# Earlier double casts and a regrouped set-up in a lightweight convolution followed by a maxout layer

## The chip, the cores and the metric

The kernel runs on one core of one Trainium2 chip. The metric is the device time of one execution in microseconds. Ten runs of the kernel before had a median of 466.01 us (464.97 to 468.08).

## The reference

Two layers follow each other. The first is a causal convolution over seven tokens with one row of seven softmax weights for each of eight heads of 24 channels; the second takes the largest of three products and multiplies it by an output matrix:

```
w   = softmax(weight, axis=-1)                  # 8 heads x 7 taps
y   = sum over k of w[h, k] * x[b, s + k - 6, h, :]   # zeros before a sequence
h   = max(y @ w1, y @ w2, y @ w3)               # 192 -> 768
out = h @ w_out                                 # 768 -> 192
```

x has 8 sequences of 4160 tokens with 192 channels in float32, so 33,280 tokens; the output has the same shape.

## The kernel before

**Blocks.** The tokens are cut into 65 blocks of 512 (eight for each sequence, and one block of the eight remainders of 64). For each block there are four kinds of work. *Load and cast*: `load_x` (L139) brings a block of x into one of seven float32 buffers (`xf`; from block 11 on only three of them, those of blocks 4, 5 and 6, take turns), and `cast_x` (L180) makes fp16 of it on POOL, into a tile `x16`. A tile `x16` holds block 4 alone, then two blocks each, and from block 13 (`QUADS`) on four. *Convolution*: `conv` (L347) multiplies bands of the taps (`band`) with `x16` on TensorE; a quad's convolution is done in two halves of four heads, in the blocks four and three ahead of the quad's first. `evac` brings it from PSUM to `ys`, `turn` transposes it by DMA into `yp`, `double` (L418) copies each half of `yp` to the other 64 partitions on POOL. *Layer 1*: `l1` (L496) makes for each block six tiles of 128 hidden channels. Since max(a, b, c) = max(a - c, b - c, 0) + c, it only needs y times (w1 - w3) and (w2 - w3), the matrices `wd`; `top` takes their larger, with a Relu on ACT and a max on DVE. The part c @ w_out becomes y times one small matrix, m = w3 @ w_out (`m16`). *Output*: `st2` (L530) multiplies h with `wo` and y with `m16`, ACT and DVE add the two lanes, `store` writes 384 KB.

**The loop.** Block t does layer 1 of block t and the output of block t - 1, interleaved. A table made ahead of the loop, `casts`, says up to which block x is cast at the start of block t; a second, `loads`, says up to which block x is loaded in block t. `casts` rises by one for each block, and by two at the blocks that a condition names (L682); `loads` follows `casts` (L683). In block t, `cast_x` stands at its start (L700); the loads stand behind the convolution's transposes on the SP queue if block t has a convolution ("late"), and otherwise behind the store of block t - 2. Each queue runs in the order in which the code was written: nothing overtakes. The convolutions stand at blocks 2, 3, 4, 6, 8, then 9 and 10 (quad 13 to 16), 13 and 14 (quad 17 to 20), and so on.

**The set-up.** The first four blocks go another way: `cast_dense` (L200) casts their x into `xz`, and `conv_dense` (L366) makes the convolution in one piece, y in `yd`, without a transpose. Its two halves, n = 0 for channels 0 to 127 and n = 1 for the rest, go to two PSUM tiles. `l1_dense` (L515) makes tiles of layer 1 for blocks 0 and 1: a "full" product over 128 rows (L522), then a "half" one over 64 rows for each lane (L526). `make_wd` (L295) subtracts w3 from w1 and w2, `copy_w3` and `cast_w3` prepare w3, `transpose_w3` (L321) transposes it on TensorE, `make_m` (L331) multiplies it with `wo`. `zero_x` (L128) clears partitions of the x buffers that no load writes. The set-up ends with the first output products of block 0 (`st2`), block 2's `conv_dense` and `make_m`; the loop's first block then has block 3's `conv_dense`.

Of the kernel before, what the change touches and what calls it, by code (L numbers as in the profile page):

```python
# [10 lines left out]
FP32 = mybir.dt.float32  # L11
FP16 = mybir.dt.float16
# [3 lines left out]
P = 128  # L16
# [12 lines left out]
def kernel(  # L29
# [95 lines left out]
        assert all(v[0] is not xf for v in xin.values())  # L125
        xin[t] = [xf, 0, ()]

    def zero_x(t):  # L128

        if t >= NDENSE:  # L130
            get_x(t)
        xf = xbuf[t]
        q0 = 0 if t >= NDENSE else NQ
        zero = idle[TOK:HALF, 0:D]
        nc.scalar.copy(out=xf[TOK:HALF, q0:NR, :],
                       in_=bass.AP(tensor=zero.tensor, offset=zero.offset,
                                   ap=[list(zero.ap[0]), [0, NR - q0], [1, D]]))

    def load_x(t, eng=nc.sync):  # L139
        if not 0 <= t < NB:  # L140
# [147 lines left out]

    w3h = const.tile([P, 2, DFF], FP16)
    wd = const.tile([P, NC + 1, DFF], FP16)  # L290
    w3t = const.tile([P, NJ, D], FP16)
    wo = const.tile([P, NJ, D], FP16)
    m16 = const.tile([P, 2, D], FP16)

    def make_wd(n, j0, j1, eng=nc.vector):  # L295
        f = slice(P * j0, P * j1)
        eng.tensor_sub(out=wd[:, n, f], in0=ws[:, n, f], in1=w3s[:, n // 2, f])
# [23 lines left out]
    def transpose_w3(g):  # L321
        ps = psw.tile([P, 2, D], FP32, tag="w", name=f"pt{g}")
        for k in range(2):
            js = slice(P * (2 * g + k), P * (2 * g + k + 1))
            for n in range(2):
                row = slice(0, HALF if n else P)
                nc.tensor.matmul(ps[:, k, P * n:min(P * (n + 1), D)], lhsT=w3h[row, n, js],
                                 rhs=ident16[row, row], start=True, stop=True)
        nc.scalar.copy(out=w3t[:, 2 * g:2 * g + 2, :], in_=ps[:])

    def make_m(i):  # L331

        ps = psp.tile([P, D], FP32, tag="p", name=f"pm{i}")
        for j in range(NJ):
            if i == 0:
                nc.tensor.matmul(ps[:], lhsT=w3t[:, j, 0:P], rhs=wo[:, j, :],
                                 start=(j == 0), stop=(j == NJ - 1))
                continue
            for e in range(2):
                nc.tensor.matmul(ps[HALF * e:HALF * (e + 1), :], lhsT=w3t[:, j, P:D],  # L340
                                 rhs=wo[:, j, :], start=(j == 0), stop=(j == NJ - 1))
        nc.scalar.copy(out=m16[:, i, :], in_=ps[:])


# [21 lines left out]
            slots[t0] = ysp.tile([P, 2, nu, 2, D], FP16, tag="ys", name=f"ys_{t}")  # L366
        convs[t0] = G, heads[0]

    def conv_dense(t, copies, pools=((None, None),) * 2):


        yd = dense[t] = ydp.tile([P, NC, NBLK], FP16, tag="yd", name=f"yd_{t}")
        for n, slots_ in enumerate(((0, 1, 2, 3), (4, 5, 4, 5))):
            pool, tag = pools[n]
            ps = (pool or psw).tile([P, NBLK], FP32, tag=tag or "w", name=f"D{n}_{t}")
            for (q, b, row_lo, rlen, lo, hi, cc) in chunks_of[t]:
                for v in range(2):
                    for g, s in enumerate(slots_):
                        h = (32 * s + 31 * v) // GRP
                        nc.tensor.matmul(  # L380
                            ps[32 * g:32 * g + 32, lo:hi],
                            lhsT=xz[t][v][0:rlen, q, 32 * s:32 * s + 32],
                            rhs=band[0:rlen, h, cc:cc + hi - lo],
                            start=(v == 0), stop=(v == 1), tile_position=(0, 32 * g))
            copies[n](out=yd[:, 2 * n, :], in_=ps[:])
# [49 lines left out]
    def y_all(t, i, c):  # L435
        if t < NDENSE:
            return dense[t][HALF * i:HALF * (i + 1), side(i, c), :]
        a = y_row(t, i)
        s0, s1, s2, s3 = (spot(t, i, c, r) for r in range(4))
        assert s3 - s2 == s1 - s0  # L440
        return bass.AP(tensor=a.tensor, offset=a.offset + P * s0,
                       ap=[list(a.ap[0]), [P * (s2 - s0), 2], [P * (s1 - s0), 2], [1, P]])
# [69 lines left out]
        op(lambda: top(t, j, ps))  # L512
        emit()

    def l1_dense(tiles):  # L515

        meet()
        ps = {}
        for t, j, pools in tiles:
            for i, (pool, tag) in enumerate(pools):  # L520
                ps[t, j, i] = pool.tile([P, NBLK], FP32, tag=tag, name=f"l{tag}{i}_{t}_{j}")
                nc.tensor.matmul(ps[t, j, i][:], lhsT=wd[:, i, P * j:P * (j + 1)], rhs=dense[t][:, 0, :],  # L522
                                 start=True, stop=False)
        for t, j, _ in tiles:
            for i in range(2):
                nc.tensor.matmul(ps[t, j, i][:], lhsT=w_of(i, NC - 1, j), rhs=y_all(t, i, NC - 1),  # L526
                                 start=False, stop=True)
        return [lambda t=t, j=j: top(t, j, (ps[t, j, 0], ps[t, j, 1])) for t, j, _ in tiles]

    def st2(t, upto):  # L530

# [89 lines left out]
    WW = ((psw, "w"), (psw, "w"))  # L621
    WPWQ = ((psw, "w"), (psp, "p"), (psw, "w"), (psq, "q"))
    ACT, DVE = nc.scalar.copy, nc.vector.tensor_copy
    make_wd(0, 0, 2)
# [17 lines left out]
    copy_w3(ACT, 2, 6)  # L642
    make_wd(2, 2, 6)
    a, b = l1_dense([(1, 0, WW), (1, 1, PQ)])
    cast_w3(2, 6)
    a()
    b()
    transpose_w3(0)
    nc.gpsimd.tensor_copy(out=wo[:], in_=wos[:])
    cast_dense(2, (nc.gpsimd.tensor_copy, nc.gpsimd.tensor_copy))  # L650
    for f in l1_dense([(0, 2, PQ), (0, 3, WW)]):
        f()
    zero_x(0)
    for f in l1_dense([(1, 2, PQ), (1, 3, WW)]):
        f()
    zero_x(1)
    transpose_w3(1)
    for f in l1_dense([(0, 4, PQ), (0, 5, WW)]):
        f()
    transpose_w3(2)  # L660
    for f in l1_dense([(1, 4, WW), (1, 5, PQ)]):
        f()
# [115 lines left out]
```

## Time and profile before

| | |
|---|---|
| median of ten runs | 466.01 us |
| the profiled execution, its own time | 467.33 us |
| its span, first to last instruction | 465.5 us |
| mean granted TensorE clock | 0.987 |
| TensorE (PE) busy | 451.7 us, 97% |
| VectorE (DVE) busy | 358.7 us, 77% |
| ScalarE (ACT) busy | 322.6 us, 69% |
| GpSimd (POOL) busy | 200.5 us, 43% |
| queue of data transfers | 70.75 MB, 65.1% of 16 engines' span |
| queue of instructions | 61 packets, 1.00 MB |

All times in a profile count from the first instruction. PE is the matmul, PEld the load of its weights, SPq the queue on which SyncE issues DMAs. In a row of the timeline the columns are start, duration, engine, line, operation, the tiles (written <- read), the shape of written <- read, and how many; in brackets stands how long the engine was idle before it and what ended that. "Issue" there means that the profile shows nothing that the engine waited for. In a row of stretches the columns are the stretch, its length, the busy time (and number) of PE, PEld, DVE, ACT and POOL, the mean granted clock, the share of the DMA engines' time and GB/s. In a row of waits stand the total, how often, and the longest.

### The profile page before, as it was taken

Reading aid. Unit: us, or ns where it says so; the run is one execution under the profiler, and the core shown is the slowest. Engines: PE = TensorE matmul, PEld = TensorE weight load, DVE = VectorE, ACT = ScalarE, POOL = GpSimd, SP = SyncE. Lnnn points to the kernel's source line nnn. Section 1 sums busy time; section 2 is a strip of 40 time slices with the busy share of each in tenths; the row PEclk is TensorE's granted clock in tenths of the full one; section 3 lists DMA queues with packets and bytes.
Section 4 is the critical chain, followed back from the end, with each engine's and each line's share of the span. In section 5 each row is a group of like instructions: output and inputs, shape, how many; then the busy total and the mean of one; then the engine's idle time right before and its main releaser. Section 6 shows DMA issues by size and latency. Waiting matters only on the chain.

```text
span 465.5 us, 18644 instructions
## 1 busy us (share of the span) xinstructions
PE 451.7 (97%) x7764; PEld 415.3 (89%) x7764; DVE 358.7 (77%) x616; ACT 322.6 (69%) x610; POOL 200.5 (43%) x223
## 2 busy tenths in 40 slices
PE   8989999499999999999999999999999999999996
PEld 4369999499999999999999999999999999999996
DVE  7657877387878888787878788787887878787775
ACT  8836767266767777676767777676777767676664
POOL 2564356606546353445446452444545361425000
PEclk9989999799999999999999999999999999999999
DMA  7938967549595866949496875959487664924223
GB/s 201 216 72 189 193 163 188 147 110 226 131 188 159 180 167 145 179 135 211 119 174 158 173 189 120 187 143 213 126 158 184 155 177 117 180 77 107 60 68 105
DMA packets 127988, 72.04 MB, mean 155 GB/s; under 512 B 52064, under 2 KB 127711, under 8 KB 127903
## 3 DMA queue, kind: packets, MB, share of 16 engines
q1 hardware_dynamic: 127743, 70.75, 65.1%
q8 instruction: 61, 1.00, 1.0%
q14 instruction: 24, 0.20, 0.2%
q10 hardware_dynamic: 160, 0.10, 0.1%
HBM read 33.28 MB, written 25.56 MB: 126 GB/s over the span
## 4 chain that ended last, share of the span: by engine, by line
PE 93%; DMA 2%; issue 1%; DVE 1%; ACT 1%; POOL 0%; SPq 0%; DVEq 0%; POOLq 0%
PE po L574 35%; PE lq L505 30%; PE lp L505 21%; PE G L360 3%; DMA xf<-in_x_dram 2%; PE D L380 1%; ACT r L492 1%; PE lp L522 0%; POOL x L192 0%; PE lw L522 0%; PE lq L522 0%; PE lp L526 0%; DVE yd L391 0%; PE lw L526 0%; DVE xz L209 0%
## 5 line engine op out<-in xcount | busy, mean ns | idle before, releaser
L574 PE MATMUL po<-wo,h 64*128 64x192 f16 x3120 | 336.8, 243 | 0.1
L493 DVE TENSOR_TENSOR h<-r,lq 128x512 f16<-128x512 f16 x385 | 264.0, 686 | 89.2 <-ACT r L492 79.8
L492 ACT ACTIVATE r<-lp 128x512 f16<-128x512 f32 x385 | 229.9, 597 | 114.5 <-PE lp L505 102.6
L505 PE MATMUL lp<-yp,wd 64*128 64x512 f16 x1098 | 296.7, 377 | 0.0
L505 PE MATMUL lq<-yp,wd 64*128 64x512 f16 x1098 | 296.3, 377 | 0.0
L574 PEld LDWEIGHTS <-h 64*128 64x128 f16 x3120 | 246.9, 94 | 7.1 <-issue 4.9
L505 PEld LDWEIGHTS <-wd 64*128 64x128 f16 x2268 | 179.7, 94 | 11.8 <-issue 0.3
L192 POOL CAST x<-xf 103x768 f16<-103x768 f32 x122 | 97.5, 827 | 127.0 <-DMA xf<-in_x_dram 124.8
L574 PE MATMUL po<-m,yp 64*128 64x192 f16 x732 | 143.7, 244 | 0.0
L422 POOL COPY yp<-yp 64x1536 f16<-64x1536 f16 (+1 forms) x62 | 89.6, 1445 | 85.4 <-DMA yp<-ys 35.2
L584 DVE TENSOR_TENSOR o<-a,po 128x384 f32<-128x384 f32 (+1 forms) x132 | 71.3, 541 | 0.6 <-ACT a L583 0.6
L574 PEld LDWEIGHTS <-yp 64*128 64x128 f16 x732 | 67.5, 94 | 0.3
L583 ACT COPY a<-po 128x384 f32<-128x384 f32 (+1 forms) x132 | 61.6, 468 | 1.4 <-PE po L574 1.1
L399 ACT CAST ys<-G 128x384 f16<-128x384 f32 x61 | 26.3, 482 | 18.5 <-PE G L360 18.5
L399 DVE CAST ys<-G 128x384 f16<-128x384 f32 x61 | 31.0, 550 | 5.7 <-PE G L360 5.7
L360 PE MATMUL G<-x,band 39*32 39x192 f16 (+2 forms) x1152 | 17.7, 238 | 5.9 <-POOL x L192 5.9
L360 PEld LDWEIGHTS <-band 39*32 39x32 f16 x1152 | 11.0, 93 | 10.8 <-issue 10.8
L505 PE MATMUL lq<-yd,wd 64*128 64x512 f16 x36 | 10.3, 391 | 0.3 <-DVE yd L391 0.3
L505 PE MATMUL lp<-yd,wd 64*128 64x512 f16 x36 | 10.2, 391 | 0.0
L380 PEld LDWEIGHTS <-xz 112*32 112x32 f16 x320 | 4.9, 111 | 3.9 <-issue 2.2
L209 POOL CAST xz<-xf 112x240 f16<-112x240 f32 (+2 forms) x15 | 4.4, 333 | 8.9 <-DVE w3s L301 7.6
L380 PE MATMUL D<-band,xz 112*32 112x103 f16 (+1 forms) x320 | 5.8, 236 | 2.0 <-issue 1.9
(62 smaller groups left out, 87.1 us busy)
## 6 DMA issues: line engine op xcount, KB each, us to landing
xf<-in_x_dram SPq DMA_DIRECT2D x113, 234.0 KB
out_dram<-o SPq DMA_DIRECT2D x62, 384.0 KB
xf<-in_x_dram SPq DMA_DIRECT2D x7, 204.8 KB
xf<-in_x_dram SPq DMA_DIRECT2D x3, 420.0 KB
ws<-in_moe_w_dram SPq DMA_DIRECT2D x8, 128.0 KB
yp<-ys SPq DMA_TRANSPOSE x62
out_dram<-o SPq DMA_DIRECT2D x5, 192.0 KB
wos<-in_moe_w_out_dram SPq DMA_DIRECT2D x1, 576.0 KB
```

Of the source, the lines that this page charges most:

```text
L192: nc.gpsimd.tensor_copy(out=x16s[t0][0:K, :, :, u, r, :].rearrange("p h j c -> p j h c"), in_=xf[0:K, 4 * r:4 * r + 4, :].rearrange("p j ( ...
L209: copy(out=xz[t][v][0:rl, q0:q1, :].rearrange("p q (k c) -> p q k c", c=CYC)[:, :, :, a:b], in_=xf[0:rl, q0:q1, :].rearrange("p q (k c) -> ...
L360: nc.tensor.matmul(G[2 * (k // per) + i][TOK * j:TOK * (j + 1), k % per, :], lhsT=band[row, h, HALF * i + LAP:HALF * i + KR], rhs=x16s[t0] ...
L380: nc.tensor.matmul(ps[32 * g:32 * g + 32, lo:hi], lhsT=xz[t][v][0:rlen, q, 32 * s:32 * s + 32], rhs=band[0:rlen, h, cc:cc + hi - lo], star ...
L399: copy(out=slots[t][:, i % 2, :, :, GRP * h0:GRP * (h0 + per)].rearrange("p u r (h c) -> p h (u r) c", c=GRP), in_=G[i][:].rearrange("p h ...
L422: nc.gpsimd.tensor_copy(out=yp[HALF * i:HALF * (i + 1), 1, :, :, :, :].rearrange("p i u k n -> p (i u k n)"), in_=yp[HALF * (1 - i):HALF * ...
L492: nc.scalar.activation(out=r[:], in_=ps[0][:], func=AF.Relu)
L493: nc.vector.tensor_max(out=hs[t][:, j, :], in0=r[:], in1=ps[1][:])
L505: nc.tensor.matmul(ps[i][:], lhsT=w_of(i, c, j), rhs=y_all(t, i, c), start=(n == 0), stop=(n == NC - 1))
L574: nc.tensor.matmul(ps[b0, i][:, s % 2, :], lhsT=a, rhs=b, start=first, stop=last and (t > 0 or s % 2 == 1))
L583: nc.scalar.copy(out=a[:, ss, :], in_=ps[s0, 0][:, ss, :])
L584: nc.vector.tensor_add(out=outs[t][:, s0:s + 1, :], in0=a[:, ss, :], in1=ps[s0, 1][:, ss, :])
```

## The change

There are two parts.

**Casts and loads.** The blocks at which two blocks of x are cast instead of one are 6, 7 and 8, where they were 8 and 9. `casts` becomes 9, 10, 12, 14, 16, 17, 18 at blocks 4 to 10, from 9, 10, 11, 12, 14, 16, 17, and `loads` follows it: 10, 12, 14, 16, 17 at blocks 4 to 8, from 10, 11, 12, 14, 16. So the x of blocks 13 to 16, the first quad, is cast at blocks 7 and 8, and from block 9 on all casts and loads stand one block earlier.

**Set-up.** `l1_dense` can now make its full and half products in any order (`parts`), and keeps its PSUM tiles open between calls; `tops` does the Relu and max afterwards. The sequence of calls is written anew: full and half products of neighbouring calls stand together, `transpose_w3` and `conv_dense` can begin with either half, block 2's `conv_dense` stands ahead of `st2` of block 0, and copies and subtractions change engines. `transpose_w3` writes 128 instead of 64 columns for its second half, twice the same 64 (`w3t` is wider), so that `make_m` needs 6 products with full columns for its second half, where it had 12.

```diff
-    def zero_x(t):
+    def zero_x(t, q0=0, q1=NR, eng=None):
...
-        q0 = 0 if t >= NDENSE else NQ
+        if eng is not None:
+            eng.memset(xf[TOK:HALF, q0:q1, :], 0.0)
+            return
...
-    w3t = const.tile([P, NJ, D], FP16)
+    w3t = const.tile([P, NJ, 2 * P], FP16)
...
+    def transpose_w3(g, order=(0, 1)):
+        ps = psw.tile([P, 2, 2 * P], FP32, tag="w", name=f"pt{g}")
+        for n in order:
+            row = slice(0, HALF if n else P)
+            for k in range(2):
+                js = slice(P * (2 * g + k), P * (2 * g + k + 1))
+                unit = ident16[row, row]
+                if n:
+                    unit = bass.AP(tensor=unit.tensor, offset=unit.offset,
+                                   ap=[list(unit.ap[0]), [0, 2], [1, HALF]])
+                nc.tensor.matmul(ps[:, k, P * n:P * (n + 1)], lhsT=w3h[row, n, js],
+                                 rhs=unit, start=True, stop=True)
         nc.scalar.copy(out=w3t[:, 2 * g:2 * g + 2, :], in_=ps[:])
...
         for j in range(NJ):
-            if i == 0:
-                nc.tensor.matmul(ps[:], lhsT=w3t[:, j, 0:P], rhs=wo[:, j, :],
-                                 start=(j == 0), stop=(j == NJ - 1))
-                continue
-            for e in range(2):
-                nc.tensor.matmul(ps[HALF * e:HALF * (e + 1), :], lhsT=w3t[:, j, P:D],
-                                 rhs=wo[:, j, :], start=(j == 0), stop=(j == NJ - 1))
+            nc.tensor.matmul(ps[:], lhsT=w3t[:, j, P * i:P * (i + 1)], rhs=wo[:, j, :],
+                             start=(j == 0), stop=(j == NJ - 1))
...
-    def conv_dense(t, copies, pools=((None, None),) * 2):
+    def conv_dense(t, copies, pools=((None, None),) * 2, order=(0, 1)):
...
-        for n, slots_ in enumerate(((0, 1, 2, 3), (4, 5, 4, 5))):
+        for n in order:
+            slots_ = ((0, 1, 2, 3), (4, 5, 4, 5))[n]
...
+    def l1_dense(tiles, parts="FH"):
 
         meet()
+        for n, part in enumerate(parts):
+            for t, j, pools in tiles:
+                for i, (pool, tag) in enumerate(pools):
+                    if (t, j, i) not in open_ps:
+                        open_ps[t, j, i] = pool.tile([P, NBLK], FP32, tag=tag, name=f"l{tag}{i}_{t}_{j}")
+                        begun.discard((t, j, i))
+                    if part == "F":
+                        a, b = wd[:, i, P * j:P * (j + 1)], dense[t][:, 0, :]
+                    else:
+                        a, b = w_of(i, NC - 1, j), y_all(t, i, NC - 1)
+                    nc.tensor.matmul(open_ps[t, j, i][:], lhsT=a, rhs=b,
+                                     start=(t, j, i) not in begun, stop=(t, j, i) in begun)
+                    begun.add((t, j, i))
...
     make_wd(1, 0, 2)
+    zero_x(6, 4, NR, nc.vector)
     conv_dense(0, (ACT, DVE))
-    zero_x(6)
+    zero_x(6, 0, 4)
...
-    cast_dense(1, (nc.gpsimd.tensor_copy, ACT))
-    a, b = l1_dense([(0, 0, PQ), (0, 1, PQ)])
+    cast_dense(1, (GP, ACT))
+    make_wd(0, 2, 4)
+    l1_dense([(0, 0, PQ), (0, 1, PQ)], "F")
+    copy_w3(GP, 2, 6)
+    make_wd(2, 2, 4, nc.gpsimd)
     cast_w3(0, 2)
-    make_wd(0, 2, 4)
-    a()
-    conv_dense(1, (ACT, ACT))
+    conv_dense(1, (DVE, ACT), order=(1, 0))
     make_wd(1, 2, 4)
-    b()
+    l1_dense([(0, 0, PQ), (0, 1, PQ)], "H")
+    tops((0, 0), (0, 1))
+    l1_dense([(1, 0, WW), (1, 1, WW)], "HF")
+    tops((1, 0), (1, 1))
...
+    l1_dense([(1, 4, PQ), (1, 5, WW)], "HF")
+    tops((1, 4), (1, 5))
+    transpose_w3(2, (0, 1))
+    cast_dense(3, (GP, GP))
+    conv_dense(2, (ACT, DVE), PQ)
     cross_wd()
-    cast_dense(3, (nc.gpsimd.tensor_copy, nc.gpsimd.tensor_copy))
     cast_x(4)
-    nc.vector.memset(xbuf[2][TOK:HALF, NQ:NR, :], 0.0)
-    nc.vector.memset(xbuf[3][TOK:HALF, NQ:NR, :], 0.0)
+    cross(2)
+    zero_x(0, NQ)
+    for t in (1, 2, 3):
+        zero_x(t, NQ, NR, nc.vector)
     st2(0, (24, 24))
     meet()
-    conv_dense(2, (ACT, DVE), PQ)
-    cross(2)
     make_m(0)
     make_m(1)
...
-        casts[t] = min(NB - 1, casts[t - 1] + (2 if t in (8, 9) else 1))
+        casts[t] = min(NB - 1, casts[t - 1] + (2 if t in (6, 7, 8) else 1))
```

The order of the instructions, first on POOL in blocks 5 to 9: the casts of blocks 10 to 16 (`x_9` is the tile of blocks 9 and 10, `x_11` that of 11 and 12, `x_13` the quad's) and the doubled copies (`yp`) for the pairs of blocks from 7, 9 and 11. Each of the three x buffers has a name, here `xf_158`, `xf_217` and `xf_315`; after the change the last is `xf_230`. Before:

```order
L192 CAST x_9_1284<-xf_130 103x4x8x24 x2
L422 COPY yp_1413<-yp_1413 64x1536 x2
L192 CAST x_11_1649<-xf_158 103x4x8x24 x2
L192 CAST x_11_1649<-xf_217 103x4x8x24 x2
L422 COPY yp_1778<-yp_1778 64x1536 x2
L192 CAST x_13_2016<-xf_315 103x4x8x24 x2
L192 CAST x_13_2016<-xf_158 103x4x8x24 x2
L192 CAST x_13_2016<-xf_217 103x4x8x24 x2
L189 MEMSET xf_315 7x192
L192 CAST x_13_2016<-xf_315 103x4x8x24 x2
L422 COPY yp_2147<-yp_2147 64x1536 x2
```

After:

```order
L194 CAST x_9_1280<-xf_130 103x4x8x24 x2
L424 COPY yp_1409<-yp_1409 64x1536 x2
L194 CAST x_11_1647<-xf_158 103x4x8x24 x2
L194 CAST x_11_1647<-xf_217 103x4x8x24 x2
L194 CAST x_13_1871<-xf_230 103x4x8x24 x2
L194 CAST x_13_1871<-xf_158 103x4x8x24 x2
L424 COPY yp_1778<-yp_1778 64x1536 x2
L194 CAST x_13_1871<-xf_217 103x4x8x24 x2
L191 MEMSET xf_230 7x192
L194 CAST x_13_1871<-xf_230 103x4x8x24 x2
L194 CAST x_17_2244<-xf_158 103x4x8x24 x2
L424 COPY yp_2153<-yp_2153 64x1536 x2
```

The casts of blocks 13 and 14 now stand ahead of the doubled copy for block 9, those of 15 and 16 right behind it, and the cast of block 17 ahead of the copy for block 11.

The SP queue, from the load of block 11 (the first `xf_158`) to that of block 16, with the stores (`out_dram`) and the transposes of blocks 9 and 11 (`yp`) between. Before:

```order
L162 DMA xf_158<-in_x_dram 39x8x192 x2
L614 DMA out_dram<-o_1587 128x4x192
L413 DMA_TRANSPOSE yp_1778<-ys_1773 128x6x128 x2
L162 DMA xf_217<-in_x_dram 39x8x192 x2
L614 DMA out_dram<-o_1809 128x4x192
L162 DMA xf_315<-in_x_dram 39x8x192 x2
L162 DMA xf_158<-in_x_dram 39x8x192 x2
L614 DMA out_dram<-o_1954 128x4x192
L413 DMA_TRANSPOSE yp_2147<-ys_2142 128x6x128 x2
L162 DMA xf_217<-in_x_dram 39x8x192 x2
L162 DMA xf_315<-in_x_dram 32x192
L162 DMA xf_315<-in_x_dram 39x7x192
```

After:

```order
L164 DMA xf_158<-in_x_dram 39x8x192 x2
L164 DMA xf_217<-in_x_dram 39x8x192 x2
L624 DMA out_dram<-o_1585 128x4x192
L415 DMA_TRANSPOSE yp_1778<-ys_1773 128x6x128 x2
L164 DMA xf_230<-in_x_dram 39x8x192 x2
L164 DMA xf_158<-in_x_dram 39x8x192 x2
L624 DMA out_dram<-o_1811 128x4x192
L164 DMA xf_217<-in_x_dram 39x8x192 x2
L164 DMA xf_230<-in_x_dram 32x192
L164 DMA xf_230<-in_x_dram 39x7x192
L164 DMA xf_230<-in_x_dram 39x8x192
L624 DMA out_dram<-o_1960 128x4x192
```

Block 12's load stands behind block 11's, those of 13 and 14 behind the transposes of block 9, and those of 15 and 16 ahead of the next store, where they stood behind it and behind the transposes of block 11.

POOL in the set-up, from the last cast of block 1's x to the first of block 2's (`xf_128`). Before:

```order
L209 CAST xz_0_100<-xf_116 112x10x8
L305 CAST w3h<-w3s 128x256
L306 CAST w3h<-w3s 64x256
L297 TENSOR_TENSOR wd<-ws,w3s 128x256 x2
L305 CAST w3h<-w3s 128x512
L306 CAST w3h<-w3s 64x512
L649 CAST wo<-wos 128x1152
L209 CAST xz_0_98<-xf_128 112x10x24
```

After:

```order
L211 CAST xz_0_100<-xf_116 112x10x8
L303 COPY w3s<-w3s 64x512
L299 TENSOR_TENSOR wd<-ws,w3s 128x256
L307 CAST w3h<-w3s 128x256
L308 CAST w3h<-w3s 64x256
L299 TENSOR_TENSOR wd<-ws,w3s 128x256 x3
L307 CAST w3h<-w3s 128x512
L308 CAST w3h<-w3s 64x512
L662 CAST wo<-wos 128x1152
L211 CAST xz_0_98<-xf_128 112x10x24
```

The copy of w3 and two subtractions have come to POOL, ahead of the casts of w3, of `wo` and of block 2's x.

More of the change, by code (lines that the diff above doesn't have):

```diff
@@ L132, in zero_x @@
         xf = xbuf[t]
-        q0 = 0 if t >= NDENSE else NQ
+        if eng is not None:
+            eng.memset(xf[TOK:HALF, q0:q1, :], 0.0)
+            return
         zero = idle[TOK:HALF, 0:D]
-        nc.scalar.copy(out=xf[TOK:HALF, q0:NR, :],
+        nc.scalar.copy(out=xf[TOK:HALF, q0:q1, :],
                        in_=bass.AP(tensor=zero.tensor, offset=zero.offset,
-                                   ap=[list(zero.ap[0]), [0, NR - q0], [1, D]]))
+                                   ap=[list(zero.ap[0]), [0, q1 - q0], [1, D]]))
     def load_x(t, eng=nc.sync):
@@ L319, in w_of @@
         return wd[HALF * i:HALF * (i + 1), n, P * j:P * (j + 1)]
[L321 to L328, printed above, removed]
+    def transpose_w3(g, order=(0, 1)):
[10 more added lines that the diff above has]
+                                 rhs=unit, start=True, stop=True)
         nc.scalar.copy(out=w3t[:, 2 * g:2 * g + 2, :], in_=ps[:])
@@ L513, in l1, with tops @@
         emit()
-    def l1_dense(tiles):
+    def l1_dense(tiles, parts="FH"):
         meet()
[L518 to L528, printed above, removed]
+        for n, part in enumerate(parts):
[11 more added lines that the diff above has]
+                    begun.add((t, j, i))
+    def tops(*tiles):
+        for t, j in tiles:
+            top(t, j, (open_ps[t, j, 0], open_ps[t, j, 1]))
+    open_ps, begun = {}, set()
     def st2(t, upto):
@@ L623 @@
     ACT, DVE = nc.scalar.copy, nc.vector.tensor_copy
+    GP = nc.gpsimd.tensor_copy
     make_wd(0, 0, 2)
     make_wd(1, 0, 2)
+    zero_x(6, 4, NR, nc.vector)
     conv_dense(0, (ACT, DVE))
-    zero_x(6)
+    zero_x(6, 0, 4)
     for t in range(NDENSE, XBUF):
```

31 lines of the change are left out of this document (11 added, 20 removed).

## The prediction

> **What bounds the kernel now.** I read the page first, then who TensorE (PE) waited for, then the timeline and the stretches of the two places that this names.
>
> ```profile
> span 465.5 us, 18644 instructions
> PE 451.7 (97%) x7764; PEld 415.3 (89%) x7764; DVE 358.7 (77%) x616; ACT 322.6 (69%) x610; POOL 200.5 (43%) x223
> ...
> PE G L360 <- POOL x L192: 5.9, 1, 5.9
> PE D L380 <- issue: 1.9, 1, 1.9
> ```
>
> The matrix engine is busy for 97% of the span, and no other engine is near it. So nothing is won by making another engine cheaper: a gain is an idle stretch of PE that goes away, or half-speed clock that goes with it. Only two waits of PE are longer than 1.2 us: 5.9 us for a cast of x on POOL, and 1.9 us for nothing that a semaphore shows.
>
> The first of them in the PE timeline, with two undisturbed quad convolutions for comparison:
>
> ```profile
> 82.39 0.24 PE L574 MATMUL po<-m,yp 64*128 64x192 f16 x1
> 88.53 0.84 PE L360 MATMUL G<-x,band 39*32 39x192 f16 x32 [5.90 <-POOL x L192]
> 97.11 0.52 PE L360 MATMUL G<-x,band 39*32 39x192 f16 x32
> 116.59 0.24 PE L574 MATMUL po<-m,yp 64*128 64x192 f16 x1
> 116.76 0.52 PE L360 MATMUL G<-x,band 39*32 39x192 f16 x32
> 123.68 0.53 PE L360 MATMUL G<-x,band 39*32 39x192 f16 x32
> ...
> 82.60:85.24 2.64, 0.04 (x2) 0.06 (x1) 0.69 (x1) 0.09 (x1) 0.20 (x1) 1.00 0.82 216
> 85.24:88.53 3.29, 0.00 (x0) 0.00 (x0) 0.00 (x0) 0.00 (x0) 3.18 (x5) 0.50 0.83 257
> 88.53:92.07 3.54, 3.54 (x55) 2.92 (x56) 1.42 (x3) 1.83 (x4) 3.40 (x3) 0.50 0.02 7
> ```
>
> This is block 9, whose convolution covers blocks 13 to 16. It should have started 0.17 us after its last output product, at 82.56 (as at 116.76 after a product at 116.59), and started at 88.53: 5.97 us of idle. From 85.24 the granted clock is 0.50 and stays so until 92.07, so the work after the wait ran slowly: the next convolution came 8.58 us later (97.11 - 88.53), where the undisturbed pair is 6.92 apart (123.68 - 116.76): 1.66 us more. The wait costs 5.97 + 1.66 = **7.6 us**. The Trainium skill ("TensorE: Matmul & The Clock Gate", Part 1) says that the gate judges free-running windows of 3413 ns; the half-clock stretch of 6.83 us (85.24 to 92.07) agrees with two of them, and since such a window begins anywhere, the 1.66 may differ between executions.
>
> **The change at this place: the feed of block 16.** SP's and POOL's rows from the load of block 11 to the cast of block 16:
>
> ```profile
> 55.36 1.14 SPq L162 DMA_DIRECT2D xf<-in_x_dram  x2
> 65.95 0.96 SPq L162 DMA_DIRECT2D xf<-in_x_dram  x2
> 68.88 2.41 SPq L162 DMA_DIRECT2D xf<-in_x_dram  x4
> 79.46 3.70 SPq L162 DMA_DIRECT2D xf<-in_x_dram  x5
> ...
> 63.16 1.60 POOL L192 CAST x<-xf 103x768 f16<-103x768 f32 x2
> 70.97 1.60 POOL L192 CAST x<-xf 103x768 f16<-103x768 f32 x2 [6.21 <-DMA xf<-in_x_dram]
> 72.63 2.99 POOL L422 COPY yp<-yp 64x1536 f16<-64x1536 f16 x2
> 75.69 3.14 POOL L192 CAST x<-xf 103x768 f16<-103x768 f32 x4
> 85.03 1.60 POOL L192 CAST x<-xf 103x768 f16<-103x768 f32 x2 [6.21 <-DMA xf<-in_x_dram]
> 86.58 0.25 POOL L189 MEMSET xf<- 7x192 f32 x1
> 86.89 1.59 POOL L192 CAST x<-xf 103x768 f16<-103x768 f32 x2
> ...
> xf<-in_x_dram SPq DMA_DIRECT2D x113, 234.0 KB
> out_dram<-o SPq DMA_DIRECT2D x62, 384.0 KB
> 70.00:75.00 5.00, 5.00 (x80) 4.84 (x76) 3.98 (x7) 3.42 (x8) 3.91 (x4) 1.00 0.86 226
> ```
>
> These are the loads of block 11, 12, 13 with 14, and 15 with 16; then the casts of 11, 12, the doubled copy for block 9, the casts of 13 and 14, 15, and 16. The last pair was issued at 79.46, three microseconds before it was needed. The change issues load 12 behind 11 (block 5), 13 and 14 where 12 stood (block 6), 15 and 16 where 13 and 14 stood (block 7). No load, cast or copy is added or dropped; all sizes stay.
>
> A block's load is 2 x 234 KB, at the 226 GB/s of the stretch 70 to 75 about 2.1 us; a store of 384 KB 1.7 us. Load 12, issued at 56.5, is then in by 63, while POOL is still in the doubled copy for block 7, and its cast follows that of 11: 64.8 to 66.4. Load 13 goes out at 65.95 and lands as its predecessor there did, at 70.97; load 14 (its buffer is free with cast 11, at 64.8) at 73.1. Casts 13 and 14: 70.97 to 74.7. Then POOL makes the doubled copy for block 9, 74.7 to 77.7; before, it was done at 75.6. It is needed when block 9 begins, about 2.3 us ahead of its convolution (an estimate from the two tiles, some 20 pairs of 0.11 us, that stand between), so at 80.2: hidden, with 2.5 us left.
>
> Load 15 goes out at 68.88 (its buffer is free with cast 12, 66.4). Load 16 must wait for cast 13 on the SP queue, until 72.6, and behind it on that queue waits the store of block 6, which nobody needs soon (there are three output buffers). After load 14 at 73.1 the store of block 5 (1.7), load 15 (2.1) and load 16 (2.1) put the landing of 16 at 79.0. The other way: load 16's issues end near 75.3 (3.70 - 0.96 after 72.6), and before, the second cast of the pair could begin 3.7 us after the last issue (83.16 to 86.89): again 79.0. POOL: cast 15 from 77.7 to 79.3, memset 0.25, cast 16 to **81.2**, with 82.56 as the date: 1.4 us to spare. Bounds of this: with no queueing load 16 lands by 77 and POOL's own row of work still ends at 81.2; with another load's time of delay (2.1 us) the cast ends at 82.9 and PE waits 0.3. I take no wait. From then on loads and casts stand one block earlier for good. The later quads had their casts in time before (PE's list of waits has only one such entry), and now have a block, 6.9 us, more.
>
> **The change in the set-up.** Here the second wait matters. PE, and the DMA rows around it:
>
> ```profile
> 21.65 2.50 PE L574 MATMUL po<-wo,h 64*128 64x192 f16 x48
> 24.08 1.10 PE L380 MATMUL D<-band,xz 112*32 112x103 f16 x80
> 25.11 0.67 PE L336 MATMUL pm<-wo,w3t 128*128 128x192 f16 x6
> 28.26 0.78 PE L380 MATMUL D<-band,xz 112*32 112x103 f16 x49
> 30.89 0.88 PE L380 MATMUL D<-band,xz 112*32 112x103 f16 x31 [1.86 <-issue]
> ...
> q1 hardware_dynamic: 67, 0.05, 9.7%
> q8 instruction: 1, 0.02, 3.7%
> ...
> 28.50:30.63 2.13, 0.53 (x45) 0.38 (x34) 1.07 (x3) 0.99 (x3) 0.90 (x2) 1.00 0.00 0
> 30.63:34.04 3.41, 3.15 (x111) 2.32 (x112) 1.25 (x2) 0.48 (x1) 3.35 (x5) 0.50 0.02 5
> ...
> 21.00 1.65 POOL L209 CAST xz<-xf 112x240 f16<-112x240 f32 x6 [1.23 <-DMA xf<-in_x_dram]
> 13.68 0.69 DVE L297 TENSOR_TENSOR wd<-ws,w3s 128x512 f16<-128x512 f32 x1
> 14.15 1.50 POOL L297 TENSOR_TENSOR wd<-ws,w3s 128x256 f16<-128x256 f32 x2 [2.91 <-DMA ws<-in_moe_w_dram]
> 10.30:21.00 10.70, 10.09 (x132) 4.15 (x128) 7.94 (x13) 9.62 (x18) 4.70 (x9) 1.00 0.95 222
> ```
>
> In the middle of block 3's convolution PE stands for 1.86 us with all its operands there. The page's 61 packets of the instruction queue hold 1.00 MB, 64 bytes for each of PE's 15,528 instructions, 256 to a packet; I read the wait as PE out of instructions. One such packet stands in the stretch 27.0 to 28.5 (the two queue rows), in the last but one of that view's 40 slices (28.4), behind the last packets of x; from 28.50 to 30.63 the DMA moves nothing. So the packet came when the loads of x had drained, and PE went on at 30.89. Then the clock is halved until 34.04: 3.15 us of half speed, 1.57 us lost.
>
> That makes a gate at 30.89 which the order of the set-up does not move, for the same loads go out in the same order. What happens ahead of it? The new order saves changes between 128-row and 64-row products, widens the transposes, merges 12 half-width products into 6, and moves copies and subtractions between DVE, ACT and POOL. But block 2's x lands at 21.00, and POOL needs 1.65 to cast it: 22.65, as before. POOL's longer list ends earlier than that: from 10.30 to 21.00 it is busy for 4.70 us (last row), and the change gives it a copy of w3 and two more subtractions of 0.75 (1.50 for two). Were all but the copy to begin only at 13.68, when DVE's row shows that the weights for it are there, it would end at 13.68 + 4.70 + 1.50 = 19.9. After 22.65 the new order still has block 2's convolution (1.03, from 24.08 to 25.11), the 48 output products (2.43, from 21.65 to 24.08), and what stands from 25.11 to 28.26 (the products for m, block 2's first tile and its products, 3.15 with some waiting): 29.3 at most, against 28.26 for the start of block 3's convolution before; without the waits in these pieces (some 1.0, an estimate from the idle times in the rows around) 28.3. So nothing is won ahead of the gate, and PE is there, 0.8 us into the convolution, 0.8 to 1.8 us ahead of 30.89: what is lost is covered by the wait. Twelve PE instructions fewer put the gate six pairs later in the convolution: 0.1 us. I take **0.1 us** for the whole set-up. Its bounds: if the wait vanished, 1.86 + 1.57 = 3.4 us won; if PE's start stayed at half clock one stretch of 3.4 us longer, up to 1.7 us of work more, mostly under the cover, and at most 1.5 lost.
>
> The Trainium skill ("DMA: Bandwidth & Descriptors", Queues, rings and completion order) states that a DMA engine takes turns between its queues packet by packet. By that rule the instructions would not sit behind x, the packet was only asked for late, and the gate would follow PE's own progress; here that moves it by up to the 1.0 us between 29.3 and 28.26, and the sum would be 459.3 at most, within the forecast's own range. The trace speaks against it, since the packet starts with the last of x.
>
> **Sum.** 7.6 + 0.1 = 7.7 us off the profiled execution: 467.33 to 459.6 (span 465.5 to 457.8, with 1.8 around it). The profiled execution is 1.3 us above the median of the ten shown (466.01, 464.97 to 468.08), as the second clock loss may come and go. From the median: **458.3 us**.
>
> **Rivals.**
> - *The wait shrinks only* (0.09). Load 16 waits on SP for cast 13, which waits for a load; if that one lands 3 to 4 us later than 70.97, the cast ends at 84 to 85 and PE idles 2 to 3 us, half the clock loss (0.8) with it: 461 to 462. For it: POOL's 6.21 us waits for x. Against: the 1.4 us to spare.
> - *The gate in the set-up opens* (0.09): PE arrives late or the packet early, and no half clock follows: 458.3 - 3.4 = 454.9. Against: the same loads.
> - *The cast is not earlier in effect* (0.05): the load is what binds, and two loads in a row end as late as before: 466.
> - *Slower* (0.04): the loads between 65 and 80 now stand so close that PE's instruction packets are held there as at 28.4. Each such wait costs 3.4 us, and some three packets fall in this stretch: 10.3 against 7.7, 468.6. It decides from a hold of about 5 us: 61 packets in 465.5 us leave 7.6 us for each, less some 2.5 from its start to PE's going on (28.4 to 30.9). Against: DMA was at 0.86 of its time from 70 to 75 before, and PE had no such wait.
>
> **How the numbers follow.** The forecast has 0.73. Its own range is 456.8 to 459.8 (the spread of the ten runs). The 8 in 10 reach down toward the open gate and up into the shrunk wait: 455.4 to 461.4. A difference below 0.3% (1.4 us) can't be told from none here. Faster: 0.73 + 0.09 + 0.09 = 0.91; same 0.05; slower 0.04.
>
> **What would show it.** PE's row of waits without the 5.9 us for POOL, no half clock after 34, the cast of block 16 ending near 81; the load of 16 going out near 72.6; the 1.9 us "issue" wait still ending near 30.9. It would be wrong if PE still waits for that cast, if another wait of over 1 us appears after 36 us, or if the convolution of block 3 ends before 31.

## The result, and the profile after

The changed kernel takes **455.85 us** (median of 9 runs, 454.6 to 458.44), the kernel before 466.45 us (median of 32 runs beside it, 464.16 to 468.56). The ratio is 0.978 with an interval of 0.9761 to 0.9799: 10.3 us less (9.4 to 11.1). The forecast was 458.3 us in a range of 455.4 to 461.4. The time lies inside, near its lower end: 7.7 us were forecast, and 2.6 us more were gained.

The head of the page of the kernel after, and the list of what PE waited for (us in total, times, longest us):

```profile
span 452.8 us, 18615 instructions
PE 446.8 (99%) x7758; PEld 412.4 (91%) x7758; DVE 359.0 (79%) x618; ACT 320.2 (71%) x607; POOL 202.2 (45%) x226
PEclk9999999999999999999999999999999999999999
PE D L382 <- POOL xz L211: 1.4, 1, 1.4
PE idle L252 <- DVE idle L247: 1.2, 1, 1.2
```

Both waits that the prediction spoke of are gone, the 5.9 us for the cast and the 1.9 us of "issue". What is left lies at the start of the program. In none of the 40 slices does the page show a reduced clock.

The PE timeline of the kernel after, at the two places:

```profile
21.51 1.10 PE L382 MATMUL D<-band,xz 112*32 112x103 f16 x80
22.54 2.15 PE L584 MATMUL po<-wo,h 64*128 64x192 f16 x48
24.62 1.16 PE L341 MATMUL pm<-wo,w3t 128*128 128x192 f16 x12
26.97 1.10 PE L382 MATMUL D<-band,xz 112*32 112x103 f16 x80
78.03 0.24 PE L584 MATMUL po<-m,yp 64*128 64x192 f16 x1
78.20 0.53 PE L361 MATMUL G<-x,band 39*32 39x192 f16 x32
85.13 0.53 PE L361 MATMUL G<-x,band 39*32 39x192 f16 x32
```

Block 9's convolution (78.20) now follows its last output product by 0.17 us, and the next one comes 6.93 us later, as in an undisturbed pair. In the set-up, block 3's convolution (26.97, before 28.26) runs its 80 pairs (a weight load with its matmul) in one piece.

The two profiled executions differ by 465.5 - 452.8 = 12.7 us. Of these, 7.63 are the wait in block 9 and its half clock, 1.86 + 1.57 = 3.43 the "issue" wait and its half clock, and 28.26 - 26.97 = 1.29 the earlier start of block 3's convolution; 0.35 is left. The medians differ by less, 10.6. One likely reason is that the "issue" wait isn't always there, as the experiments show.

The feed of block 16 on POOL (first 6 rows: casts of blocks 13 and 14, the doubled copy, cast of 15, the pad rows, cast of 16), and then on SP the loads of 15 and 16, in the timeline of the kernel after:

```profile
66.62 1.60 POOL L194 CAST x<-xf 103x768 f16<-103x768 f32 x2 [5.83 <-DMA xf<-in_x_dram]
69.70 1.60 POOL L194 CAST x<-xf 103x768 f16<-103x768 f32 x2 [1.48 <-DMA xf<-in_x_dram]
71.36 2.99 POOL L424 COPY yp<-yp 64x1536 f16<-64x1536 f16 x2
74.42 1.59 POOL L194 CAST x<-xf 103x768 f16<-103x768 f32 x2
75.96 0.25 POOL L191 MEMSET xf<- 7x192 f32 x1
76.27 1.59 POOL L194 CAST x<-xf 103x768 f16<-103x768 f32 x2
64.51 4.51 SPq L164 DMA_DIRECT2D xf<-in_x_dram  x5
```

Cast 16 ends at 76.27 + 1.59 = 77.86, for a convolution that begins at 78.20. Neither cast 15 nor cast 16 waits for its load: from 69.70 on POOL works without a pause.

### The profile page after: what moved, and what is told of

Same layout as the page of the kernel before. It is cut to its first block, busy times and chain, and to the rows that moved or that the text cites. A ratio compares the mean times of both kernels' runs of the same rounds, so it can differ in the third digit from the quotient of the medians.

```text
span 452.8 us, 18615 instructions
## 1 busy us (share of the span) xinstructions
PE 446.8 (99%) x7758; PEld 412.4 (91%) x7758; DVE 359.0 (79%) x618; ACT 320.2 (71%) x607; POOL 202.2 (45%) x226
## 4 chain that ended last, share of the span: by engine, by line
PE 97%; DMA 1%; SPq 1%; DVE 0%; issue 0%; POOL 0%; ACT 0%; DVEq 0%; POOLq 0%
PE po L584 37%; PE lq L507 32%; PE lp L507 22%; PE G L361 3%; DMA xf<-in_x_dram 1%; PE D L382 1%; PE lw L530 1%; PE lp L530 1%; SPq L227 0%; PE lq L530 0%; SPq L223 0%; PE pm L341 0%; SPq L164 0%; DVE h L495 0%; POOL xz L211 0%
## 5 line engine op out<-in xcount | busy, mean ns | idle before, releaser
L530 PEld LDWEIGHTS <-wd 128*128 128x128 f16 (+1 forms) x48 | 3.1, 97 | 5.5 <-issue 3.1
```

The lines of the kernel that those rows point to most:

```text
L530: nc.tensor.matmul(open_ps[t, j, i][:], lhsT=a, rhs=b, start=(t, j, i) not in begun, stop=(t, j, i) in begun)
```

## The experiments

The theory going in: the change has two separate parts. The casts give what the wait and its half clock cost. The set-up gives little by itself, and whether the "issue" wait is there differs. The rivals: the set-up is what gave the 2.6 us that were not forecast, or the "issue" wait has gone because the new order moved it.

### Each part alone, and both kernels again

`casts_alone` is the kernel before with the new table of doubled casts:

```diff
-        casts[t] = min(NB - 1, casts[t - 1] + (2 if t in (8, 9) else 1))
+        casts[t] = min(NB - 1, casts[t - 1] + (2 if t in (6, 7, 8) else 1))
```

> The set-up of before with the new table of casts. Theory (the cast and its half clock cost 7.6 us, the set-up brings the rest): 466.4 - 7.6 = 458.9 us, PE's wait of 5.9 us for POOL gone, the cast of block 16 done 1 us or more ahead of its convolution, and the wait without a semaphore near 30 us still there with a half clock behind it. Rival (the casts bring it all, and the set-up nothing): 455.9 us.

`setup_alone` is the kernel after with the old table:

```diff
-        casts[t] = min(NB - 1, casts[t - 1] + (2 if t in (6, 7, 8) else 1))
+        casts[t] = min(NB - 1, casts[t - 1] + (2 if t in (8, 9) else 1))
```

> The new set-up with the old table of casts. Theory: the gain left over, 3.0 us, so 463.4 us, with PE's 5.9 us wait for POOL still there and no wait without a semaphore near 30 us. Rival (the set-up brings nothing): 466.4 us.

`before_again` and `after_again` are the two kernels unchanged, for a second profile of each.

> The kernel before once more, for a second look at the set-up. If the wait near 29 to 31 us belongs to this order of work, it is here again, ending within 1 us of 30.9; if it came from one slow execution's transfers, it is gone or much shorter.

> The changed kernel once more. If the new set-up passes the point of the wait for its own reasons, there is again no wait of PE over 1.5 us after 10 us, and the loads of x end before 26.5 us; if it was luck of one execution, the wait is back and ends near 30 us.

| kernel | median, us | runs | ratio to before | "issue" wait, us | half clock after 20 us |
|---|---|---|---|---|---|
| casts_alone | 457.03 | 5 | 0.9808 (0.9779 to 0.9837) | none | none |
| setup_alone | 464.15 | 12 | 0.9954 (0.993 to 0.9978) | 2.33 | 31.49 to 34.91, 86.11 to 92.93 |
| before_again | 466.76 | 1 | | 0.49 | 82.65 to 92.89 |
| after_again | 456.51 | 1 | | 0.79 | none |

The casts are worth 466.66 x 0.0192 = **9.0 us** (7.6 to 10.3) against 7.6 in the sum. The set-up is worth 2.1 us (1.0 to 3.3) alone; on top of the casts it is 10.3 - 9.0 = 1.3 us, a difference that the two intervals, which overlap, do not resolve. In the sum it was 0.1.

The time of `casts_alone` lies between its theory (458.9 us) and its rival (455.9), and that of `setup_alone` near its theory (463.4 against 466.4). What was expected of the "issue" wait failed in both: it is absent in `casts_alone`, where it was to stay, and there in `setup_alone`, where it was to be gone. In `before_again` it is much shorter than 1.86 us, and in `after_again` it has come back, short.

Why the casts give more than 7.6 stands in the second profile of the kernel before. The timeline of `before_again` at the same place, PE, then SP's issue of loads 15 and 16 and POOL's cast of 15:

```profile
79.47 0.24 PE L574 MATMUL po<-m,yp 64*128 64x192 f16 x1
86.66 0.84 PE L360 MATMUL G<-x,band 39*32 39x192 f16 x32 [6.94 <-POOL x L192]
96.55 0.53 PE L360 MATMUL G<-x,band 39*32 39x192 f16 x32
76.54 3.60 SPq L162 DMA_DIRECT2D xf<-in_x_dram  x5
83.17 1.60 POOL L192 CAST x<-xf 103x768 f16<-103x768 f32 x2 [6.74 <-DMA xf<-in_x_dram]
```

Its stretches there (busy time of PE, PEld, DVE, ACT and POOL, the granted clock, DMA share, GB/s):

```profile
82.65:86.66 4.01, 0.00 (x1) 0.00 (x0) 0.00 (x0) 0.00 (x0) 3.37 (x5) 0.50 0.60 198
86.66:92.89 6.23, 6.23 (x73) 5.13 (x74) 2.86 (x5) 2.42 (x5) 4.52 (x4) 0.50 0.00 0
```

Worked as in the prediction: 86.66 - 79.47 - 0.17 = 7.02 us of idle, and 96.55 - 86.66 = 9.89 to the next convolution, 2.97 above 6.92: **10.0 us**. The idle time is longer because the load of block 15 took longer. SP issued it at 76.54, and POOL could cast at 83.17, 6.63 us later; in the profile before it was 79.46 and 85.03, 5.57 us. And the half clock lasted 10.24 us (82.65 to 92.89) instead of 6.83: three stretches of 3.41 instead of two, 6.23 us of it with work. The same place in `setup_alone`, and its "issue" wait:

```profile
26.51 0.82 PE L382 MATMUL D<-band,xz 112*32 112x103 f16 x55
29.66 0.48 PE L382 MATMUL D<-band,xz 112*32 112x103 f16 x25 [2.33 <-issue]
81.57 0.24 PE L584 MATMUL po<-m,yp 64*128 64x192 f16 x1
88.06 0.84 PE L361 MATMUL G<-x,band 39*32 39x192 f16 x32 [6.24 <-POOL x L194]
97.29 0.53 PE L361 MATMUL G<-x,band 39*32 39x192 f16 x32
```

Here it is 6.32 of idle and 9.23 - 6.92 = 2.31: 8.6 us. The three profiles give 7.6, 8.6 and 10.0, with a mean of 8.8, and the timed price is 9.0 (7.6 to 10.3). So the forecast took one execution's price, the lowest of the three, for that of the median.

The new order of the set-up does not take the "issue" wait away: it is there in `setup_alone` with 2.33 us, longer than in the profile before, and absent in `casts_alone` with the old order. What the order does change is PE's progress. From `casts_alone`:

```profile
24.44 1.10 PE L380 MATMUL D<-band,xz 112*32 112x103 f16 x80
27.94 1.10 PE L380 MATMUL D<-band,xz 112*32 112x103 f16 x80
76.98 1.59 POOL L192 CAST x<-xf 103x768 f16<-103x768 f32 x2
79.18 0.52 PE L360 MATMUL G<-x,band 39*32 39x192 f16 x32
```

With the old order block 3's convolution begins at 28.26, 27.73 and 27.94 in three profiles, with the new one at 26.97, 26.81 and 26.51: 1.2 us earlier. The two groups do not overlap; I take this as the set-up's steady gain. The last two rows show the cast of 16 in time here too, 0.6 us ahead of its convolution, where 1 us or more was expected.

### What the "issue" wait hangs on: extra_load and late_load6

In every profile where PE stops there, it stops at the same instruction. 959 matmuls and weight loads have started, and the 960th is held (the expectations call the place the 961st, which starts together with it): after 49 pairs of block 3's convolution in the old order, after 55 in the new. It went on 2.5 to 3.1 us after the third packet of the instruction queue had started. The prediction took it that this packet goes out when the loads of x have drained. `extra_load` makes the loads last longer, with one more load, into a tile that nobody reads:

```diff
+    spare = const.tile([P, NR, D], FP32, name="spare")
+    for i in range(2):
+        nc.sync.dma_start(out=spare[HALF * i:HALF * i + KR, :, :],
+                          in_=bass.AP(tensor=x.tensor, offset=(SEQ + NBLK * (i + 1)) * D,
+                                      ap=[[D, KR], [TOK * D, NR], [1, D]]))
```

> The changed kernel with one more load of 2 x 234 KB, into a tile that nothing reads, behind the load of block 6. Theory (PE's third packet of instructions waits behind the loads of x): that packet starts about 2 us later than the 24.9 and 25.8 us of the two looks at the changed kernel, near 27 to 28, and PE, which has used up its instructions near 27.3 us, waits 2 to 3 us in block 3's convolution, at the same 961st instruction, with a half clock behind it or not. Rival (a DMA engine takes turns between its queues, so the data does not hold the instructions): the packet starts where it did, and PE waits no longer than 0.8 us there.

It took 456.63 us, one run (`after_again` 456.51). PE timeline of `extra_load`:

```profile
26.93 0.82 PE L382 MATMUL D<-band,xz 112*32 112x103 f16 x55
28.92 0.48 PE L382 MATMUL D<-band,xz 112*32 112x103 f16 x25 [1.17 <-issue]
```

Its DMA queues (packets, MB, share of 16 engines; q1 carries the data, q8 PE's instructions), first in the stretch 26 to 27, then in 28 to 29:

```profile
q1 hardware_dynamic: 259, 0.19, 86.6%
q8 instruction: 1, 0.02, 8.0%
...
q1 hardware_dynamic: 232, 0.17, 65.8%
```

The packet started at 26.34, among 259 data packets, and 232 more followed in 28 to 29. So it does not wait until the loads have drained: that reading falls. But the wait is not gone either: at 1.17 us it lies between the theory's 2 to 3 us and the rival's 0.8.

`late_load6` takes the last load of x, that of block 6, away from there and issues it behind block 2's cross copy:

```diff
-    zero_x(6, 4, NR, nc.vector)
...
-    for t in range(NDENSE, XBUF):
+    for t in range(NDENSE, XBUF - 1):
...
     cross(2)
+    zero_x(6, 4, NR, nc.vector)
+    load_x(6)
```

> The changed kernel with the load of block 6 held back until the DVE has cleared its buffer behind block 2's copies, near 25 us; the half of that clearing that DVE does moves there. Theory: the third packet of instructions starts 1.5 to 2 us earlier, near 23.5, PE never waits in block 3's convolution, and the time is 0 to 1.5 us less than that of the changed kernel, 455 us. Rival (the data does not hold the instructions): the packet stays near 25, the time too.

It took 455.31 us (6 runs, 454.3 to 456.21), a ratio of 0.9762 (0.9732 to 0.9792). Its PE timeline:

```profile
26.36 1.10 PE L382 MATMUL D<-band,xz 112*32 112x103 f16 x80
```

And its DMA queues in the stretch 23 to 24:

```profile
q1 hardware_dynamic: 105, 0.07, 26.1%
q8 instruction: 1, 0.02, 7.3%
```

With the data traffic thinner (26.1% of the DMA's time) the packet started at 23.15, the earliest of all profiles, and PE did not stop, as the theory of this run had it. The time is lower than the kernel after by 0.5 us in the median, but the intervals overlap: it is not shown to be faster.

Over the profiles, the packet's start and the start of PE's 959th matmul or weight load, the last one ahead of the place, tell when the wait comes:

| profile | packet starts | PE at its 959th | wait, us |
|---|---|---|---|
| before | 28.43 | 28.82 | 1.86 |
| before_again | 26.33 | 28.28 | 0.49 |
| casts_alone | 25.68 | 28.47 | none |
| after | 24.90 | 27.58 | none |
| after_again | 25.84 | 27.42 | 0.79 |
| setup_alone | 26.61 | 27.12 | 2.33 |
| extra_load | 26.34 | 27.54 | 1.17 |
| late_load6 | 23.15 | 26.97 | none |

PE waits where the packet starts less than about 2.6 us ahead of it, and not otherwise. The four profiles of the next section fit too: three have leads of 2.89, 3.37 and 3.74 us and no wait, and the timed one of `st2_first`, with a lead of 2.35 us, has a stop of 0.2 us. If the packet is asked for 256 instructions ahead, PE was at that place between 24.5 and 24.8 with the old order and between 22.1 and 22.7 with the new, and in these eight profiles the packet started 0.8 to 4.4 us later. From that place PE took 3.6 to 4.4 us to its 959th with the old order and 4.9 with the new, so the new order leaves the packet more time, and in three of its five profiles here the packet was still too late. That the packet is asked for there is an inference. How long it is held does not simply follow the data traffic: 0.8 us in `casts_alone` and 1.0 in `late_load6`, where the traffic was thinning, but 3.9 in `before`, where it thinned out too, and 1.5 in the first profile of `ungrouped`, where 324 data packets started in the same microsecond. What decides it stays open.

### Which part of the new order gives the 1.2 us: st2_first and ungrouped

`st2_first` puts block 2's convolution and its cross copy back behind the 48 output products of block 0:

```diff
-    conv_dense(2, (ACT, DVE), PQ)
     cross_wd()
     cast_x(4)
-    cross(2)
...
     st2(0, (24, 24))
     meet()
+    conv_dense(2, (ACT, DVE), PQ)
+    cross(2)
```

> The changed kernel with block 2's convolution and its copies back behind block 0's output products. If this place in the order is what brings PE to block 3's convolution earlier (26.5 to 27.0 us against 27.7 to 28.3 before), it comes there 1 us later, near 28; if the regrouped products do it, the start stays within 0.3 us of 26.8.

> The kernel after with the convolution of block 2 and its cross copy back behind the 48 output products of block 0, timed. In the one profile so far its convolution of block 3 began at 30.0 instead of 26.8, but PE also ran at half clock until 17.4 instead of 8.7 to 11.0, and was 2.95 us late already at the first transposes. Theory A (the late start is the clock's, which differs between executions whatever the order): the median is within 1 us of the kernel after, a ratio to before of 0.976 to 0.981, and a profile whose clock is full by 11 has block 3's convolution at 26.8 to 27.3. Theory B (the order of these two pieces is worth the 3 us): ratio 0.981 to 0.985, block 3's convolution at 29 to 30 whatever the clock does.

`ungrouped` lets transposes and products alternate between 128 and 64 rows again:

```diff
-    l1_dense([(1, 0, WW), (1, 1, WW)], "HF")
+    l1_dense([(1, 0, WW), (1, 1, WW)], "FH")
...
-    transpose_w3(0, (1, 0))
+    transpose_w3(0)
```

and the same for the calls of blocks 4 and 5 of the hidden units, with `k` outside `n` in `transpose_w3`.

> The changed kernel with full before half products in every call, and the transposes taking turns between 128 and 64 rows again; all else stays. There are 9 more changes of kind: theory (about 0.09 us each, the difference of 0.30 and 0.21 us between neighbouring starts): block 2's convolution starts 0.8 us later than in the changed kernel (21.0 to 21.5 us). Rival (POOL's or ACT's work sets the pace there): less than 0.3 us.

> The kernel after with the transposes and the set-up's products alternating between 128 and 64 rows again, timed. Theory A (grouping saves some 0.3 us at each of three groups of transposes, little elsewhere, 0.6 in all by the one profile): block 3's convolution begins at 27.1 to 27.6, and the ratio to before is 0.977 to 0.981, not to be told from the kernel after. Theory B (grouping is the whole of the set-up's gain): block 3's convolution at 27.9 to 28.3 as before, ratio 0.980 to 0.984, as with the casts alone.

| kernel | single run, us | timed median, us | ratio to before |
|---|---|---|---|
| st2_first | 457.74 | 456.52 (4 runs) | 0.98 (0.9769 to 0.9831) |
| ungrouped | 455.0 | 457.4 (6 runs) | 0.9811 (0.9778 to 0.9844) |

The times do not tell these two from the kernel after (0.9761 to 0.9799). The timelines do, once one thing is set aside: the first profile of `st2_first` ran at half clock until 17.43, and the timed profile of `ungrouped` from 11.00 to 14.41, so both were late before their own part began. So I measure from the first four transposes to block 3's convolution; what a change did ahead of these transposes is not in that figure. These two rows from `after_again`:

```profile
15.48 0.49 PE L333 MATMUL pt<-ident,w3h 64*128 64x128 f16 x4
26.81 0.82 PE L382 MATMUL D<-band,xz 112*32 112x103 f16 x55
```

From the first profile of `st2_first`, and (last row) from its timed one:

```profile
18.43 0.49 PE L333 MATMUL pt<-ident,w3h 64*128 64x128 f16 x4
30.01 1.10 PE L382 MATMUL D<-band,xz 112*32 112x103 f16 x80
27.16 1.29 PE L382 MATMUL D<-band,xz 112*32 112x103 f16 x80
```

And from the first profile of `ungrouped`:

```profile
15.40 0.71 PE L333 MATMUL pt<-ident,w3h 128*128 128x128 f16 x4
27.37 1.10 PE L382 MATMUL D<-band,xz 112*32 112x103 f16 x80
```

That piece is 11.33 us in `after_again`, and also in `after`, `setup_alone` and `late_load6` (11.51 in `extra_load`). It is 11.58 and 11.70 in the two profiles of `st2_first`, and 11.97 and 11.91 in those of `ungrouped`. By these rows the grouping is worth 0.6 us and the order of the two pieces 0.3; together they are 0.9 of the 1.2 us. Four transposes in one group take 0.49 us where the alternating ones take 0.71. The rest, 0.3 us, was not tried by itself. The large difference in the first profile of `st2_first` was the clock's: the timed profile, with the full clock from 8.27, has block 3's convolution at 27.16 (theory A). For `ungrouped`, block 2's convolution came 21.85 - 15.40 = 6.45 us after the first transposes against 21.51 - 15.64 = 5.87 in `after`: 0.6 us later, between the 0.8 of its theory and the 0.3 of the rival. Its timed profile has block 3's convolution at 28.73, which by itself would speak for theory B, but the half clock from 11.00 had made it late; the 11.91 us agree with theory A.

## Why the prediction came out as it did

**What bounds the kernel, right.** The two waits named were the ones that went, and nothing took their place: PE is busy for 99% of the span. The size came out less well. Of the 2.6 us that were not forecast, 9.0 - 7.6 = 1.4 come from the price of the wait and 1.3 - 0.1 = 1.2 from the set-up. The range reached down to 455.4 for another reason, an opened gate, so that the time lies inside it owes something to luck.

**The price of the wait, right in kind and too small.** The term "The wait costs 5.97 + 1.66 = 7.6 us" measures 9.0 us (7.6 to 10.3). Both parts vary between executions: the idle time with the landing of the loads (5.97, 6.32, 7.02), the half clock with the place of the stretches of 3.41 us (1.66, 2.31, 2.97). By the free-running windows of the Trainium skill ("TensorE: Matmul & The Clock Gate", Part 1) this second part was to vary, and the traces agree: 6.83, 6.83 and 10.24 us of half clock are two, two and three times 3.41. The prediction said so of the half clock, and put into the sum the one value that it had, which turned out the lowest.

**The feed of block 16, right, with less to spare.** Load 16 had to wait for cast 13. Taken from block 9's convolution, load 16 was to go out 82.56 - 72.6 = 9.96 us ahead of it; cast 13 ended 78.20 - 68.22 = 9.98 ahead. Load 13's landing was put 11.59 us ahead and was 11.58. Only load 14 was mis-sized: 2.1 us behind load 13 in the prediction, 3.08 on the chip (69.70 - 66.62; 2.54 in `casts_alone`). POOL then worked without a pause, as forecast, and cast 16 ended 0.34 us ahead of the convolution instead of 1.4. The stretches of the kernel after around it (the last two columns are the DMA's share and GB/s):

```profile
62.00:66.00 4.00, 4.00 (x64) 3.90 (x61) 2.97 (x6) 2.88 (x6) 0.00 (x0) 1.00 0.81 179
66.00:70.00 4.00, 4.00 (x65) 3.88 (x63) 3.26 (x6) 2.89 (x6) 1.91 (x3) 1.00 0.83 234
70.00:75.00 5.00, 5.00 (x132) 4.63 (x130) 4.16 (x8) 3.51 (x8) 4.81 (x5) 1.00 1.09 252
```

From 62 to 66 the DMA moved 179 GB/s, not the 226 that the prediction reckoned with, which would make load 14 late; that this is the cause is argued, not shown. The rival of a shrunk wait missed coming true by 0.34 us in this profile.

**The slower rival, wrong.** Whatever PE's instruction packets met between 65 and 80 us, it cost nothing: with the DMA at 0.83 to 1.09 of its time (0.96 from 75 to 80) PE has no idle time there.

**The set-up, wrong.** Two steps failed. The first is "block 2's x lands at 21.00 ... So nothing is won ahead of the gate". The landing was that of one execution: in the kernel after POOL begins block 2's cast at 19.22, and in `casts_alone`, with the old order, at 19.23:

```profile
19.22 3.25 POOL L211 CAST xz<-xf 112x240 f16<-112x240 f32 x12
19.23 1.64 POOL L209 CAST xz<-xf 112x240 f16<-112x240 f32 x6 [1.01 <-DMA xf<-in_x_dram]
```

So PE's own work sets the pace there, and the shorter work reaches block 3's convolution 1.2 us sooner. The second is "a gate at 30.89 which the order of the set-up does not move, for the same loads go out in the same order". The gate is real, at the same count of PE's instructions, six pairs later in the new order, as said; but PE went on at times from 28.0 to 30.9 where it closed, and in six of twelve profiles, `casts_alone`, `after` and `late_load6` among them, it did not close. By the prediction's own test ("if the convolution of block 3 ends before 31") it was wrong: that ended at 26.97 + 1.10 = 28.07.

So the profile after looks like the rival of an opened gate (454.9, chance 0.09), but the "issue" wait still comes and goes with either order, so its 3.4 us are no gain of the change. Two of the ten executions of the changed kernel (458.44 and 456.27 us) have a mean granted clock of 0.996 against 0.999 or 1.0 in the others. One stretch of 3.41 us at half clock in 455 us would give 0.996; which wait it followed is not known. The gain is 9.0 us from the casts, and by the medians 1.3 to 2.1 from the set-up, of which the timelines account for 1.2.

On what the packet waits for, the prediction set the Trainium skill ("DMA: Bandwidth & Descriptors", Queues, rings and completion order: a DMA engine takes turns between its queues packet by packet) against the trace and followed the trace, which had the packet start with the last of x. That was one coincidence: `extra_load` has it start in the middle of the data, which agrees with the skill's rule. The rule alone does not explain the up to 4.4 us from the place where it would be asked for to its start.

## What to carry to other kernels

Take the price of a stall from several executions before it goes into a sum: its idle part moves with the landing of a load, and its half clock with where the stretches of 3.41 us fall, so the same wait cost 7.6, 8.6 and 10.0 us. A landing time seen once is no bound for what comes ahead of it: ask what the engine's own work would allow if the data came 2 us sooner. And a wait seen in one profile ("issue", 1.9 us) may be absent in the next one of the same kernel, so the gain of removing it is its mean, not its size.

## What the runs showed of the hardware

- PE stopped for 0.2 to 2.3 us in the middle of a convolution with its operands there, in six of twelve profiles, always before its 960th matmul or weight load, and only where the third packet of the instruction queue started less than about 2.6 us ahead of PE. It resumed 2.5 to 3.1 us after the packet's start.
- An idle time of 1.86 or 2.33 us brought one stretch of 3.41 us at half clock; waits of 0.2 to 1.2 us at the same place brought none.
- The clock's start varies too: it was full from 7.6 to 11.0 us on in most profiles, but from 17.4 us in one, and in another it fell back from 11.0 to 14.4. In the first of these, a layer-1 product over 512 columns took 0.63 us before 17 us and 0.38 after it, and block 3's convolution came 2.9 us later than in the other execution of the same kernel (30.01 and 27.16).
- Transposes that change between 128 and 64 rows cost more than grouped ones: four alternating ones took 0.71 us, four grouped ones 0.49.
